# A polysketch attention and mixture-of-experts kernel: the second matmul of the mixture by Strassen's seven half products, its sums on GpSimd, and a rebuilt beginning

## Chip, cores, metric

One core of one Trainium2 chip; float32 in and out. The metric is device time in microseconds of the whole program, median of several executions. The program uses one core.

## The reference, cut to what matters

```python
# attention: B, H, S, D = 4, 4, 1088, 32; r = 8
#   phi(x) = outer product of S1 x and S2 x, 64 features; num / den by k_p, v and z sums
# its result, (B*S, H*D) = (4352, 128), is the x of the mixture
N, D, E, F = 4352, 128, 4, 1024
p = domain_probs / (domain_probs.sum(-1, keepdims=True) + 1e-09)
for e in range(E):
    h = np.maximum(x @ w1[e], 0.0)          # first matmul
    out += p[:, e:e + 1] * (h @ w2[e])      # second matmul
```

Hidden units come in 32 blocks of 128 (4 experts of 8). Per block and chunk of tokens the kernel makes hp = w1 x on TensorE, hid = max(hp, 0) * gate on VectorE, and adds w2 hid to an accumulator in PSUM on TensorE.

## The kernel before

Tokens are columns. Every 128x128 product is issued as two *half products* of 64 outputs each, on two column tiles of the array (I call them the two *sides*).

```python
def product(out, weights, moving, **flags):
    for r in (slice(0, 64), slice(64, P)):
        nc.tensor.matmul(out[r, :], weights[:, r], moving, **flags)
# ...
def first(i):
    m, kk = steps[i]                       # chunk, block
    hp = ps_h.tile([P, 512], F32, tag="h", name="hp")          # 2 buffers
    product(hp[:, 0:n], w1_sb[:, e, P * f : P * f + P], xT[chunks[m]][:, 0:n], start=True, stop=True)
    hid[i] = mpool.tile([P, CW], F32, tag="hid", bufs=4, name="hid")
    nc.vector.scalar_tensor_tensor(out=hid, in0=hp, scalar=0.0, in1=gate, op0=ALU.max, op1=ALU.mult)  # APs cut
def second(i):
    product(acc[m][:, 0:n], w2_sb[:, e, f, :], hid.pop(i)[:, 0:n], start=(kk == 0), stop=(kk == NK - 1))
# ...
for i in range(len(steps) + LA):           # LA = 2: second() runs two blocks behind first()
    first(i); second(i - LA); next(pieces, None)     # cut: conditions
```

`pieces` is a generator with the attention work of later chunks: each `next` issues one attention instruction (or a few on TensorE) among the mixture's. I call one such issue a *piece*. The names qp, qa, qf, qb (query features), kp (key features), yz and ev (the additions at the end of a chunk after the change) will turn up in the profiles below; gate is the weight of an expert for each token. In this kernel GpSimd makes the key products and is otherwise idle.

## Time and profile before

| | before |
|---|---|
| median in the first measurement (3 executions) | 537.84 us |
| span of the profile | 534.7 us |
| first hp | 27.1 us |
| from first hp to last acc | 504.0 us, TensorE busy 503.3 |
| busy PE / VectorE / GpSimd | 97% / 62% / 5% |

In the lines of the profile PE is TensorE, PEld its weight loads, DVE VectorE, ACT ScalarE, POOL GpSimd; L570 is line 570 of the kernel that ran; `a <- b` in a wait means that a stood still until b was done. "Busy" of TensorE counts the recorded, overlapping passes.

### The profile page before, as it was taken

To read this page: it belongs to the slowest core of one execution; us is meant where nothing else is said; L and a number is where in the kernel's file an instruction comes from. 1 tells how busy PE (TensorE), PEld (TensorE's weight loads), DVE (VectorE), ACT (ScalarE), POOL (GpSimd) and SP (SyncE) were. 2 spreads that over 40 slices of the span, in tenths; PEclk is the share of its full clock that TensorE was granted. 3 is DMA by queue.
4 is the path that set the end of the run, shared out by engine and by line. 5 is a ranking of instruction groups with operands and counts; after the bars stand their busy time and mean duration, and the time that the engine had idled before them with its cause. 6 is when DMAs were issued, how large, how long until landed. Compare 5 with 4: busy or idle time off the path is not lost.

```text
span 534.7 us, 9910 instructions
## 1 busy us (share of the span) xinstructions
PE 518.1 (97%) x4197; PEld 287.0 (54%) x4197; DVE 333.5 (62%) x788; ACT 25.3 (5%) x56; POOL 26.1 (5%) x80
## 2 busy tenths in 40 slices
PE   3799999999999999999999999999999999999997
PEld 1677776555554445544554445454555444444896
DVE  3878874777647645367866754447875664654554
ACT  1210000000000001000000000100000000000000
POOL 2240000000000004000000000400000000000000
PEclk9999999999999999999999999999999999999999
DMA  7492502002015002000202001100301000100100
GB/s 209 109 276 103 157 28 71 0 1 73 1 49 139 2 0 77 1 1 8 67 2 63 1 0 23 53 1 0 75 1 31 12 1 10 26 1 2 16 9 8
DMA packets 32893, 22.82 MB, mean 43 GB/s; under 512 B 21200, under 2 KB 29520, under 8 KB 32848
## 3 DMA queue, kind: packets, MB, share of 16 engines
q1 hardware_dynamic: 31536, 21.78, 14.7%
q8 instruction: 33, 0.54, 0.4%
q10 hardware_dynamic: 1312, 0.40, 0.4%
q14 instruction: 12, 0.10, 0.1%
HBM read 19.87 MB, written 2.31 MB: 41 GB/s over the span
## 4 chain that ended last, share of the span: by engine, by line
PE 95%; DVE 2%; DMA 1%; issue 1%; ACT 0%; SPq 0%; DVEq 0%; ACTq 0%
PE hp L141 44%; PE acc L141 44%; PE nd L141 3%; PE kv L141 1%; PE qc L141 1%; PE kf L141 1%; PE wp L146 1%; DMA kn<-in_k_dram 1%; DVE kp L287 1%; DVE den L399 0%; DMA vn<-in_v_dram 0%; DVE qp L374 0%; DVE fs L279 0%; DVE hid L492 0%; ACT den L389 0%
## 5 line engine op out<-in xcount | busy, mean ns | idle before, releaser
L492 DVE SCALAR_TENSOR_TENSOR hid<-hp,gate 128x384 f32<-128x384 f32 (+4 forms) x448 | 213.4, 476 | 185.4 <-PE hp L141 176.8
L141 PE MATMUL hp<-xT,w_sb 128*64 128x384 f32 (+4 forms) x1792 | 311.5, 426 | 1.2 <-DVE xT L404 1.0
L141 PE MATMUL acc<-hid,w_sb 128*64 128x384 f32 (+4 forms) x1792 | 311.0, 425 | 0.0
L141 PEld LDWEIGHTS acc<-hid,w_sb 128*64 128x64 f32 x1792 | 128.6, 137 | 106.9 <-issue 68.7
L141 PEld LDWEIGHTS hp<-xT,w_sb 128*64 128x64 f32 x1792 | 126.8, 137 | 106.0 <-issue 62.6
L287 POOL TENSOR_TENSOR kp<-fs 128x128 f32<-128x128 f32 (+1 forms) x56 | 22.6, 443 | 310.9 <-DVE fs L279 310.9
L399 DVE RECIPROCAL den<-den 128x128 f32<-128x128 f32 (+1 forms) x37 | 32.3, 876 | 0.2 <-ACT den L389 0.2
L389 ACT ACTIVATE den<-nd,eps 64x384 f32<-64x384 f32 (+4 forms) x28 | 14.4, 514 | 359.3 <-issue 313.4
L374 DVE TENSOR_TENSOR qp<-qa,qb 64x384 f32<-64x384 f32 (+4 forms) x56 | 26.6, 474 | 1.3
L141 PE MATMUL nd<-qp,kvz 128*64 128x384 f32 (+4 forms) x112 | 17.6, 427 | 0.7 <-DVE kvz L312 0.7
L371 DVE STREAM_SHUFFLE qa<-qf 128x384 f32<-128x384 f32 (+4 forms) x28 | 14.0, 502 | 0.0
L404 DVE TENSOR_TENSOR xT<-nd,den 64x384 f32<-64x384 f32 (+4 forms) x28 | 13.2, 473 | 0.5
L141 PEld LDWEIGHTS kv<-vx,kp 128*64 128x64 f32 (+1 forms) x288 | 11.9, 137 | 3.0 <-issue 2.0
L141 PE MATMUL kv<-vx,kp 128*64 128x66 f32 (+3 forms) x288 | 13.0, 238 | 0.0
L146 PE MATMUL wp<-warm 128*128 128x512 bf16 x13 | 4.3, 501 | 9.0 <-ACT warm L119 9.0
L141 PEld LDWEIGHTS nd<-qp,kvz 128*64 128x64 f32 x112 | 8.0, 137 | 8.0 <-issue 4.5
L141 PE MATMUL qc<-qT,sq 128*64 128x384 f32 (+4 forms) x56 | 9.8, 426 | 1.5 <-DVE fs L279 1.5
L141 PEld LDWEIGHTS kf<-sk,kT 128*64 128x64 f32 x144 | 8.2, 137 | 3.9 <-issue 2.6
L141 PE MATMUL kf<-sk,kT 128*64 128x128 f32 x144 | 9.8, 275 | 0.5 <-DVE fs L279 0.5
L354 DVE STREAM_TRANSPOSE qT<-qn 128x384 f32<-128x384 f32 (+4 forms) x14 | 6.9, 493 | 2.9 <-DMA qn<-in_q_dram 2.9
L146 PEld LDWEIGHTS <-warm 128*128 128x128 bf16 x13 | 1.5, 124 | 11.3 <-ACT warm L119 9.0
L274 ACT COPY fs<-kf 128x256 f32<-128x256 f32 (+1 forms) x12 | 3.8, 319 | 77.5 <-PE kf L141 77.5
(59 smaller groups left out, 64.5 us busy)
## 6 DMA issues: line engine op xcount, KB each, us to landing
gate<-gates SPq DMA_DIRECT2D x6, 768.0 KB, 4.3
w_sb<-in_moe_w_dram SPq DMA_DIRECT2D x8, 512.0 KB, 8.9
gate<-gates SPq DMA_DIRECT2D x4, 640.0 KB, 4.3
kn<-in_k_dram SPq DMA_DIRECT2D x4, 544.0 KB, 4.1
qn<-in_q_dram SPq DMA_DIRECT2D x4, 544.0 KB, 3.9
vn<-in_v_dram SPq DMA_DIRECT2D x28, 64.0 KB, 3.9
out_dram<-ob SPq DMA_DIRECT2D x24, 48.0 KB, 1.8
gate<-gates SPq DMA_DIRECT2D x2, 384.0 KB, 5.4
```

Source lines behind the costliest of these rows:

```text
L141: nc.tensor.matmul(out[r, :], weights[:, r], moving, **flags)
L146: nc.tensor.matmul(wp[:, :], warm[:, 0:P], warm[:, :], start=True, stop=True)
L274: nc.scalar.copy(fss[b][:, t0 : t0 + n, :], _ap(kf, 0, P, 0, [[P, n], [1, H * R2]]))
L287: eng.tensor_tensor(out=_ap(kps[b], 0, P, 256 * t0 + P * (h // 2) + 64 * x + 32 * (h % 2), [[256, n], [R, 4], [1, R]]), in0=_ap(fss[b], 0, ...
L354: nc.vector.transpose(qT[:, 0:n], qn[b][:, 32 * g0 : 32 * g0 + n])
L371: nc.vector.stream_shuffle(in_=qf[:, 0:n], out=qa[:, 0:n], mask=mask_a[x])
L374: nc.vector.tensor_tensor(out=qp[p][64 * x : 64 * x + 64, 0:n], in0=qa[64 * p : 64 * p + 64, 0:n], in1=qb[64 * p : 64 * p + 64, 0:n], op=A ...
L389: nc.scalar.activation(den[64 * p : 64 * p + 64, 0:n], nd[p][64 - 64 * p : 128 - 64 * p, 0:n], ACTF.Identity, bias=eps[64 * p : 64 * p + 6 ...
L399: nc.vector.reciprocal(den[:, s : s + w], den[:, s : s + w])
L404: nc.vector.tensor_tensor(out=xT[b, ch][r, 0:n], in0=nd[p][r, 0:n], in1=den[r, 0:n], op=ALU.mult)
L492: nc.vector.scalar_tensor_tensor(out=_ap(hid[i], 0, P, 0, [[32, n // 32], [1, 32]]), in0=_ap(hp, 0, P, 0, [[32, n // 32], [1, 32]]), scala ...
```

## The change

The intent: Strassen's scheme multiplies two 2x2 block matrices with seven block products for eight. Here the four weight blocks are two hidden blocks by two halves of the outputs, and the four blocks of hid are two hidden blocks by two halves of the columns. TensorE saves an eighth of the second matmul; in return there are four sums of weight blocks (once for each expert, GpSimd), four sums of hid blocks at every step (a *step* is now a pair of hidden blocks), and some additions at the end of a chunk (`gather`). The seven half products alternate between the two sides.

```diff
-    NK = E * FB
-    WIDTHS = [[192, 256, 320, 320], [384, 384, 320], [384, 384, 320], [384, 384, 192, 128]]
+    NQ = E * FB // 2
+    CHUNKS = [256, 416, 416] + [512] * 6 + [192]      # the last one stays plain
...
+    def first(i, work):
+        for j in range(2):
+            hp = psum(ps_h, "h")                       # 3 buffers
+            both(hp[:, 0:n], w1_sb[:, e, c : c + P], xT[...], start=True, stop=True)
+            nc.vector.scalar_tensor_tensor(out=hid[i] block j, in0=hp, in1=gate, ...)
+            work()                                     # a piece of attention
+        if plain(m):
+            return
+        nc.gpsimd.tensor_tensor(out=ts[:, 0:2, 0:w], in0=..., in1=..., op=ALU.subtract)   # two sums in one
+        nc.gpsimd.tensor_tensor(out=ts[:, 2, 0:w], in0=hid[i][:, 1, w:n], in1=ts[:, 0, 0:w], op=ALU.subtract)
+        (nc.vector if i % 2 else nc.gpsimd).tensor_tensor(
+            out=ts[:, 3, 0:w], in0=hid[i][:, 1, 0:w], in1=ts[:, 2, 0:w], op=ALU.subtract
+        )
...
+        todo = (      # second(): by side, (weights, moving); 3 or 4 of each are used in turn
+            [(blk(0, 0), hb(0, 0)), (new(3), hb(1, 1)), (blk(0, 1), hb(1, 0)), (new(1), tb(2))],
+            [(new(2), tb(1)), (new(0), tb(0)), (blk(1, 1), tb(3)), (new(1), tb(2))],
+        )
```

Cut from it: the beginning (the warm-up of TensorE no longer waits for ScalarE, q comes before v, query features of the first chunk as three replicated products in place of shuffles, key products straight from PSUM, some of them on GpSimd), the division (two 32x32 transposes around a small reciprocal), later key products on VectorE, chunks of 512, and the buffers that follow. The line with `nc.vector if i % 2` I call the *fourth sum*. In odd steps VectorE makes it, in the order of its program, ahead of the next step's hids, and it needs GpSimd's sums.

## The prediction

> **What bounds the kernel now.** I read the page first, its busy line and its chain.
>
> ```profile
> PE 518.1 (97%) x4197; PEld 287.0 (54%) x4197; DVE 333.5 (62%) x788; ACT 25.3 (5%) x56; POOL 26.1 (5%) x80
> ...
> PE 95%; DVE 2%; DMA 1%; issue 1%; ACT 0%; SPq 0%; DVEq 0%; ACTq 0%
> PE hp L141 44%; PE acc L141 44%; PE nd L141 3%; PE kv L141 1%; PE qc L141 1%; PE kf L141 1%; PE wp L146 1%; DMA kn<-in_k_dram 1%; DVE kp L287 1%; DVE den L399 0%; DMA vn<-in_v_dram 0%; DVE qp L374 0%; DVE fs L279 0%; DVE hid L492 0%; ACT den L389 0%
> ```
>
> TensorE is 95% of the chain that ends last, half of it each in the two mixture products, hp and acc. Busy alone does not prove saturation, so I asked for three stretches: the mixture, the end and the beginning (columns: PE, PEld, DVE, ACT, POOL busy).
>
> ```profile
> 27.10:531.10 504.00, 503.32 (x4032) 276.79 (x4032) 316.51 (x725) 19.72 (x42) 18.93 (x48) 1.00 0.13 37
> 531.10:534.80 3.70, 0.00 (x0) 0.00 (x0) 0.32 (x1) 0.00 (x0) 0.00 (x0) 0.88 0.12 18
> 0.00:27.10 27.10, 14.78 (x167) 10.19 (x167) 16.63 (x62) 5.61 (x14) 7.19 (x32) 1.00 0.58 158
> ```
>
> So the span is 27.1 us of beginning, 504 us in which TensorE never rests, and a tail of 3.7. The pace inside the middle comes from the timeline of TensorE:
>
> ```profile
> 300.42 0.81 PE L141 MATMUL hp<-xT,w_sb 128*64 128x384 f32 x4
> 301.07 0.81 PE L141 MATMUL acc<-hid,w_sb 128*64 128x384 f32 x4
> 301.71 0.81 PE L141 MATMUL hp<-xT,w_sb 128*64 128x384 f32 x4
> 302.36 0.81 PE L141 MATMUL acc<-hid,w_sb 128*64 128x384 f32 x4
> ```
>
> One 128x128 product of 384 columns is two half products (64 outputs each), recorded as two passes each, and the next begins 0.645 us later with no gap. The beginning, TensorE alone:
>
> ```profile
> 8.99 4.30 PE L146 MATMUL wp<-warm 128*128 128x512 bf16 x13 [8.99 <-ACT warm L119]
> 13.22 2.47 PE L141 MATMUL kf<-sk,kT 128*64 128x128 f32 x36
> 17.24 0.55 PE L141 MATMUL qc<-qT,sq 128*64 128x192 f32 x4 [1.55 <-DVE fs L279]
> 17.59 4.82 PE L141 MATMUL kv<-vx,kp 128*64 128x132 f32 x72
> 23.10 1.06 PE L141 MATMUL nd<-qp,kvz 128*64 128x192 f32 x8 [0.69 <-DVE kvz L312]
> 24.09 1.97 PE L141 MATMUL kf<-sk,kT 128*64 128x128 f32 x32
> 27.09 0.87 PE L141 MATMUL hp<-xT,w_sb 128*64 128x192 f32 x8 [1.03 <-DVE xT L404]
> ```
>
> The warm-up waits until 8.99 for a ScalarE instruction that stands behind the v loads in ScalarE's queue; everything follows from there.
>
> **What the Trainium skill says.** "TensorE: Matmul & The Clock Gate", section Back-to-back issue gap, gives N/2.4 + 2.5 ns for a warm matmul. The trace agrees if a pass of float32 counts two cycles a column: means of 486 ns at 384 columns and 273 at 128 differ by 0.832 ns a column, 2/2.4, and 0.645 us for four passes on two column tiles is 2 x (320 + 2.5). "TensorEngine Tiling (Array Packing)", section Key Properties, says that different tiles can execute weight loads and matmuls in parallel; that 0.645 us holds four passes of over 320 ns each agrees. "GPSIMD Engine Reference", section 3.1, has 4497 ns for a two-input add of 2048 elements, 2.2 ns an element. "SBUF — State Buffer", section Who interferes with whom, says that a VectorE instruction with two SBUF inputs contends with a GpSimd one that reads SBUF. The groups by form bear on both:
>
> ```profile
> L287 POOL TENSOR_TENSOR kp<-fs 128x160 f32<-128x160 f32 x28 | 12.2, 471 | 0.3 <-DVE fs L279 0.3
> L287 POOL TENSOR_TENSOR kp<-fs 128x128 f32<-128x128 f32 x28 | 10.6, 416 | 310.6 <-DVE fs L279 310.6
> L492 DVE SCALAR_TENSOR_TENSOR hid<-hp,gate 128x384 f32<-128x384 f32 x192 | 106.8, 556 | 117.6 <-PE hp L141 116.2
> L287 DVE TENSOR_TENSOR kp<-fs 128x160 f32<-128x160 f32 x4 | 2.0, 567 | 0.0
> ```
>
> GpSimd shows (471-416)/32 = 1.72 ns an element, a little better than the page. VectorE's two-input kp, run beside GpSimd's, takes 567 ns for 160 elements, as long as its 384-column hid, whose other input is PSUM: contention, as the page says.
>
> **The change, part by part.** A half product of n columns costs its side 2 x (0.833 n + 2.5) ns, from the above; a side is one column tile, and both run at once.
>
> *First product*, kept: 32 blocks x 4352 columns x 1.667 ns = 232.1 us, plus 10 chunks x 32 x 2 x 2.5 ns = 1.6: 233.7.
> *Second product*: 16 pairs of blocks, each seven half products of n/2 columns, 3.5 a side, in place of eight. On 4160 tokens: 16 x 3.5 x 2080 x 1.667 ns = 194.1 us, plus 9 x 16 x 7 x 2.5 ns = 2.5: 196.6. The last 192 tokens stay plain: 10.4. Together the mixture is 440.7 us.
> *Before, the same sum*: 64 x 4352 x 1.667 = 464.2, plus 14 x 64 x 2 x 2.5 ns = 4.5: 468.7. **Saved on TensorE: 28 us**, 7/8 of one product, little lost to the shorter matmuls. As TensorE never rests there, this counts whole if no other engine takes over.
>
> *Attention inside the mixture*: 5 ns a token (qc one product, nd two), kf 2.0 and kv 2.6 us a batch (2 x 1.3 by the timeline). Before: 896 tokens, one batch without kf, two whole: 32.6. After: 832 tokens and three whole batches: 34.5. Check on before: 27.1 + 468.7 + 32.6 = 528.4 against 531.1 read, so 2.7 us escape this count (row-tile changes in kv, waits between); I carry them over.
>
> *VectorE*: a hid of 512 columns, by the slope (556-291)/256 = 1.035 ns from the 384 and 128 forms, takes 690 ns, 320 instructions in all and some 195 us against 213. Added: one of four sums in every second step (about 0.42 us at 256 columns, 72 times, 30 us), the gathering of nine chunks (about 2.9 us each, 26 us), key products moved from GpSimd. The division gets cheaper: 32 us of den reciprocals become two transposes. About 380 us in a span near 505: not a bound by busy time.
> *GpSimd*: at 512 columns a step takes a sum of 512 elements (416 + 384 x 1.72 = 1.08 us), one of 256 (0.64) and, in even steps, a third: 2.0 us mean against a step of 2 x 0.858 + 3.5 x 0.432 = 3.2 us on TensorE. Not the bound, and with second() two steps behind first() the chain hid, three sums (about 2.5 us after the last hid) has nearly 5 us before TensorE wants it.
>
> *Beginning*: the warm-up no longer waits for ScalarE. kn landed at 5.2 and the three kT transposes ended at 6.6, with sk to be had by then: kf starts near 7 instead of 13.2. The three replicated query products cost 2.6 us of TensorE but take the shuffles away. Estimate: kf to 9.5, query products to 12.2, kv to 14.8, nd 16.3, division 17.7. The first gates have to pass behind 1.5 MB of weights, so I put the first hp, or the first hid that really goes through, at **19.8**, 7.3 us earlier, though with the first kf of batch 1 no longer tucked in.
>
> Sum: 19.8 + 440.7 + 34.5 + 2.7 carried + 3.3 for new waits + 3.7 tail = 504.7 us of span. The median stands 3.1 over the span of the profile (537.84 to 534.7), so **508 us**, 5.6% faster.
>
> **Rivals.** (1) *VectorE becomes the bound by its order.* In odd steps it does the fourth sum itself and must wait for GpSimd's two, about 1.5 us of standing still after the last hid. Two steps: 4 hid at 0.61 (issue spacing), 0.34 for the sum, some 1.5 of attention, 0.3 gathering, 1.5 waiting, 0.3 contention, 6.4 us against 7.0 of TensorE with its attention. Close: if contention adds 0.5 us an instruction instead, VectorE rules while attention is dense (about seven chunks, 56 pairs of steps) and 30 us could shrink to 10: 525. For it speak the 567 ns above; against it, that hid has one SBUF input and that most waits fall into slack. (2) *The first chunk starves.* At 256 columns a step is 1.63 us, while GpSimd has 1.27 plus weight sums of 0.64: 1.9 in the steps that have one. Worth 1 to 4 us, of which I counted about 2: 511 at worst. (3) *Pairing breaks.* Seven is odd and sides alternate across steps; were two neighbours to land on one side, or different moving data on two sides to slow each other, the 8-for-7 gain of 28 us would go: 536. The code alternates without exception; no case of two different streams exists in this trace, except in time between products. (4) *Beginning hidden anyway*: gates or v arrive late and hp starts at 25: 513.
>
> **Range and chances.** All waits hidden and hp at 18 gives 500; rival 1 by half, or 2 and 4 together, 517. So 500 to 517. Faster by over 2% means under 527.3, which only rival 1 in full with another, or 3, prevents: 0.94 faster, 0.05 same, 0.01 slower.
>
> **What would show it.** acc becomes 2016 recorded passes of 256, 208 and 128 columns beside the plain ones, starting on each side every 216 ns at 256; TensorE busy over 97% from first hp to last acc; first hp between 18 and 21; GpSimd busy near 290 us (96 steps of 2.0, 32 of 1.8, 16 of 1.3, weight sums and beginning 20); VectorE 360 to 410 with idle before the fourth sum near 1.5 us. I am wrong if waits of TensorE on sums or hid add up to more than 10 us, if GpSimd's 512-element sum takes over 1.6 us, or if the acc passes at 256 start more than 230 ns apart.

## The result

| | before | after |
|---|---|---|
| median, same measurement (4 executions each) | 537.77 us | 558.0 us |
| ratio, 95% interval | | 1.038 (1.036 to 1.040) |
| first hp / first hid | 27.1 / 27.7 us | 16.9 / 20.4 us |
| VectorE, GpSimd busy | 333, 26 us | 344, 350 us |

Ratios are the mean time of one kernel's fast runs over that of the other's of the same rounds, so not quite the ratio of the medians. The kernel became 20 us slower where 30 us faster was predicted. The page after, busy line and chain:

```profile
PE 512.1 (92%) x4178; PEld 301.8 (54%) x4178; DVE 344.4 (62%) x736; ACT 27.8 (5%) x67; POOL 349.8 (63%) x414
...
POOL 44%; DVE 31%; PE 17%; issue 4%; DMA 2%; POOLq 0%; DVEq 0%; SPq 0%
POOL sums L570 24%; DVE hid L557 16%; POOL sums L576 13%; PE h L169 8%; PE o L169 7%; POOL sums L577 6%; DVE sums L577 4%; PE f L169 3%; DVE qp L393 2%; DVE yz L661 1%; DVE ev L672 1%; DMA gates<-pt 1%; DVE qa L451 1%; DVE ob L635 1%; DMA gate<-gates 1%
```

TensorE went from 95% of the chain to 17%; GpSimd and VectorE share three quarters of it, with the sums and the hids, though each of them is busy for less than two thirds of the span. Two engines that are each a third idle and yet fill the chain in turn: that is the picture of a hand-over, not of a full engine. The three stretches, as before (window in us, its length, PE, PEld, DVE, ACT, POOL busy with the number of instructions, granted clock, DMA share, GB/s):

```profile
16.90:552.90 536.00, 498.67 (x3988) 292.99 (x3988) 332.86 (x685) 23.19 (x54) 338.38 (x372) 0.99 0.13 36
552.90:556.70 3.80, 0.16 (x1) 0.00 (x0) 0.38 (x1) 0.00 (x0) 0.00 (x0) 1.00 0.16 26
0.00:16.90 16.90, 13.22 (x190) 8.78 (x190) 11.20 (x50) 4.57 (x13) 11.38 (x42) 1.00 0.71 206
```

The beginning is 10 us shorter; the middle has 37 us in which no pass is running at all. Who waits for whom there (total us, times, longest):

```profile
DVE sums L577 <- POOL sums L576: 169.8, 72, 3.8
POOL sums L570 <- DVE hid L557: 154.8, 88, 5.3
...
PEld h L169 <- DVE hid L557: 58.9, 58, 2.9
...
PE h L169 <- DVE hid L557: 19.7, 23, 2.4
```

VectorE stands still for the fourth sum 72 times, 2.36 us on average; GpSimd stands still for hid nearly as long (154.8 us in 88 waits); and TensorE waits for hid, because hp has three PSUM buffers and only a hid frees one. It hardly waits for sums: only some 2.5 us of its waits name them. One turn late in the kernel, where no attention is left, first GpSimd and then VectorE (start, length, and in brackets the idle time before):

```profile
470.42 1.27 POOL L570 TENSOR_TENSOR sums<-hid 128x512 f32<-128x512 f32 x1 [1.74 <-DVE hid L557]
471.77 0.73 POOL L576 TENSOR_TENSOR sums<-hid,sums 128x256 f32<-128x256 f32 x1
472.58 0.72 POOL L577 TENSOR_TENSOR sums<-hid,sums 128x256 f32<-128x256 f32 x1
473.26 1.27 POOL L570 TENSOR_TENSOR sums<-hid 128x512 f32<-128x512 f32 x1
474.61 0.73 POOL L576 TENSOR_TENSOR sums<-hid,sums 128x256 f32<-128x256 f32 x1
477.08 1.28 POOL L570 TENSOR_TENSOR sums<-hid 128x512 f32<-128x512 f32 x1 [1.74 <-DVE hid L557]
```
```profile
469.66 1.96 DVE L557 SCALAR_TENSOR_TENSOR hid<-h,gate 128x512 f32<-128x512 f32 x3
475.37 0.43 DVE L577 TENSOR_TENSOR sums<-hid,sums 128x256 f32<-128x256 f32 x1 [3.75 <-POOL sums L576]
475.71 1.88 DVE L557 SCALAR_TENSOR_TENSOR hid<-h,gate 128x512 f32<-128x512 f32 x3
```

Five sums of two steps follow each other on GpSimd (470.42 to 475.34). VectorE is done with its hids at 471.62, stands still for 3.75 us before the fourth sum, does it at 475.37, then makes the next hids, and only after the second of them may GpSimd begin again, at 477.08. The turn is closed: 4.92 us of GpSimd and 1.74 in which VectorE works and GpSimd waits, **6.66 us for two steps**, and none of it can start before the part ahead of it has ended. TensorE needs 2 x 3.23 = 6.45 us for two steps, by the prediction's pace; so even without attention the turn is the longer, and every piece, gathering addition or conflict between the two engines inside it makes it longer still: from fourth sum to fourth sum the last three turns of chunk 8 took 6.64 to 6.67 us, those of chunks 3 to 7 7.4 to 7.8 on average. I call it the **ring**.

TensorE's own part is as predicted. Four lines of its timeline in the same kernel, two passes that start together and the two that follow:

```profile
387.10 0.38 PE L169 MATMUL o<-sums,w2s 128*64 128x256 f32 x1
387.11 0.38 PE L169 MATMUL o<-hid,w2s 128*64 128x256 f32 x1
387.32 0.38 PE L169 MATMUL o<-sums,w2s 128*64 128x256 f32 x1
387.33 0.38 PE L169 MATMUL o<-hid,w_sb 128*64 128x256 f32 x1
```

Passes of 256 columns start on both sides together, with different weights and different moving data, and the next pair 0.216 us later.

Two theories went to the chip. **Ring**: the order of the fourth sum on VectorE closes a cycle between two in-order engines, and its length sets the time. **Throughput**: GpSimd, at 350 us busy, and its conflicts with VectorE's two-input instructions are simply too much. (That the sums reach TensorE too late was a third.) The first calls for a change of order, the second for less work.

### The profile page after: what moved, and what is told of

Read it like the earlier page. It is cut to its first block, busy times and chain, and to the rows that moved or that the text cites. A ratio compares the mean times of both kernels' runs of the same rounds, so it can differ in the third digit from the quotient of the medians.

```text
span 556.7 us, 9898 instructions
## 1 busy us (share of the span) xinstructions
PE 512.1 (92%) x4178; PEld 301.8 (54%) x4178; DVE 344.4 (62%) x736; ACT 27.8 (5%) x67; POOL 349.8 (63%) x414
## 4 chain that ended last, share of the span: by engine, by line
POOL 44%; DVE 31%; PE 17%; issue 4%; DMA 2%; POOLq 0%; DVEq 0%; SPq 0%
POOL sums L570 24%; DVE hid L557 16%; POOL sums L576 13%; PE h L169 8%; PE o L169 7%; POOL sums L577 6%; DVE sums L577 4%; PE f L169 3%; DVE qp L393 2%; DVE yz L661 1%; DVE ev L672 1%; DMA gates<-pt 1%; DVE qa L451 1%; DVE ob L635 1%; DMA gate<-gates 1%
## 5 line engine op out<-in xcount | busy, mean ns | idle before, releaser
L169 PE MATMUL h<-xT,w_sb 128*64 128x512 f32 (+3 forms) x1280 | 315.9, 536 | 25.0 <-DVE hid L557 19.7
L570 POOL TENSOR_TENSOR sums<-hid 128x512 f32<-128x512 f32 (+2 forms) x144 | 177.4, 1232 | 158.8 <-DVE hid L557 154.8
L169 PE MATMUL o<-sums,w2s 128*64 128x256 f32 (+2 forms) x864 | 208.8, 359 | 1.2 <-POOL w2s L473 1.2
L557 DVE SCALAR_TENSOR_TENSOR hid<-h,gate 128x512 f32<-128x512 f32 (+3 forms) x320 | 186.9, 599 | 29.9 <-PE h L169 24.8
L169 PEld LDWEIGHTS h<-xT,w_sb 128*64 128x64 f32 x1280 | 120.7, 137 | 115.8 <-DVE hid L557 58.9
L169 PE MATMUL o<-hid,w_sb 128*64 128x256 f32 (+3 forms) x704 | 178.5, 353 | 0.0
L169 PEld LDWEIGHTS o<-sums,w2s 128*64 128x64 f32 x864 | 115.3, 137 | 53.7 <-issue 27.0
L577 DVE TENSOR_TENSOR sums<-hid,sums 128x256 f32<-128x256 f32 (+2 forms) x72 | 31.3, 434 | 169.8 <-POOL sums L576 169.8
L576 POOL TENSOR_TENSOR sums<-hid,sums 128x256 f32<-128x256 f32 (+2 forms) x144 | 102.2, 710 | 11.3
L169 PEld LDWEIGHTS o<-hid,w_sb 128*64 128x64 f32 x704 | 92.4, 137 | 20.3 <-issue 13.6
L169 PE MATMUL o<-hid,w2s 128*64 128x256 f32 (+2 forms) x288 | 79.8, 359 | 0.8 <-POOL w2s L473 0.8
L577 POOL TENSOR_TENSOR sums<-hid,sums 128x256 f32<-128x256 f32 (+2 forms) x72 | 52.3, 726 | 5.7
```

Of the source, the lines that this page charges most:

```text
L169: nc.tensor.matmul(out(s), weights(s), moving(s), **flags)
L557: nc.vector.scalar_tensor_tensor(out=_ap(hid[i], 0, P, CW * j, [[32, n // 32], [1, 32]]), in0=_ap(hp, 0, P, 0, [[32, n // 32], [1, 32]]), ...
L570: nc.gpsimd.tensor_tensor(out=ts[:, 0:2, 0:w], in0=_ap(hid[i], 0, P, w, [[CW, 2], [1, w]]), in1=_ap(hid[i], 0, P, 0, [[w, 2], [1, w]]), op ...
L576: nc.gpsimd.tensor_tensor(out=ts[:, 2, 0:w], in0=hid[i][:, 1, w:n], in1=ts[:, 0, 0:w], op=ALU.subtract)
L577: (nc.vector if i % 2 else nc.gpsimd).tensor_tensor(out=ts[:, 3, 0:w], in0=hid[i][:, 1, 0:w], in1=ts[:, 2, 0:w], op=ALU.subtract)
```

## The experiments

Each run is an edit of the changed kernel. I also read the length of each chunk in each trace, from its first hid to the next chunk's first hid; the table is below.

### 1. The fourth sum deferred

```diff
-        (nc.vector if i % 2 else nc.gpsimd).tensor_tensor(out=ts[:, 3, 0:w], ...)
+        if i % 2: waiting.append(lambda: fourth(nc.vector))   # issued after the next step's two hids
+        else:     fourth(nc.gpsimd)
```

> Only the place of VectorE's fourth sum (odd steps) in its program order changes: it is issued after the two hids of the next step, so VectorE no longer stands still for GpSimd before it may make the next hids. Theory, a ring: in the changed kernel GpSimd's five sums of two steps (about 4.9 us) and then VectorE's fourth sum and two hids (about 1.7 us plus an attention instruction between them) follow each other without overlap, 6.65 us per two steps at the least and over 8 where attention is dense, against 6.45 of TensorE plus its attention. With the ring cut, TensorE is the bound again: about 505 us (500 to 515), waits of VectorE on the second sum near zero. Rival, throughput or contention of GpSimd and VectorE (350 and 344 us busy, two-input instructions blocking each other): the order of one instruction changes nothing, 545 to 558 us.

513.6 us, correct, ratio to before 0.956 (0.954 to 0.958). The same instructions in another order: 44 us less than the changed kernel. VectorE's wait on the second sum fell from 169.8 us to

```profile
DVE sums L583 <- POOL sums L580: 6.0, 6, 2.1
```

while GpSimd was busy longer (356 us) in a shorter span. Throughput as the only cause is out.

### 2. All four sums on GpSimd

```diff
-        (nc.vector if i % 2 else nc.gpsimd).tensor_tensor(
+        nc.gpsimd.tensor_tensor(
```

> The fourth sum always on GpSimd: no VectorE instruction waits for GpSimd any more, but GpSimd gets 72 more sums of 0.7 us, some 50 us more work (busy about 400 us). Ring theory: GpSimd needs 2.85 us per step of 512 columns against 3.5 of TensorE, so it is hidden: 505 to 515 us. Rival, GpSimd's throughput: it was the bound, so it gets slower: 565 us or more.

513.0 us, correct, 0.955 (0.953 to 0.957). GpSimd has 52 us more to do (402 busy) and the kernel is 45 us faster. No instruction of VectorE that lies ahead of a hid reads GpSimd's sums any more, and the chain is TensorE's again (GpSimd had 44% of it in the changed kernel):

```profile
PE 88%; POOL 7%; DMA 3%; DVE 1%; issue 1%; DVEq 0%; POOLq 0%; SPq 0%
```

The trace still puts 24 us of waits before 17 hids down to GpSimd's sums. Why was not looked into; the chunk table (experiment 8) shows no cost of them from chunk 2 on.

### 3. No sums at all

```diff
-        ts = mpool.tile(...)            # and the three instructions that fill it
-        tb = lambda a: ts[:, a, 0:w]
+        tb = lambda a: hb(a // 2, 1 - a % 2)     # slices of hid: wrong on purpose
```

> Wrong result on purpose: none of the four sums of hid is computed, the seven half products read slices of hid instead. TensorE's instructions stay the same in number and size. It measures what TensorE's part of the change is worth: if the seven half products run in pairs as predicted (28 us saved, first hp at 16.9), 500 to 505 us. Rival: TensorE itself is slower than predicted with different streams on its two column tiles: 520 or more.

503.9 us (the result is wrong, as meant), 0.938 (0.936 to 0.939). This is what TensorE, beginning, attention and gathering cost together, within the 500 to 505 expected. The prediction without its 3.3 us for new waits had 504.5.

### 4. One piece moved

```diff
-            work()                      # after each of the two hids
+            if i % 2: work()
+            elif j:   work(); work()    # even steps: both pieces after the second hid
```

> In even steps the attention instruction that stood between the two hids is issued after the second one; nothing else changes, same work on each engine. Ring theory: that one instruction lay in the ring (about 0.5 us in some 55 to 60 pairs of steps, more where it was blocked by GpSimd), so 20 to 30 us less: 528 to 540 us. Rival (throughput, contention): no work is removed, 553 to 560 us.

558.0 us: **no change**, and my expectation missed. The trace shows why the simple ring was too simple. There are two ways round. One is the five sums, fourth sum, two hids. The other is VectorE's own: four hids with all pieces ahead of the last one, then GpSimd's first two sums of the odd step, then the fourth sum. The piece lies on both; moving it behind the second hid takes it off the first way and leaves it on the other. In a dense stretch of this run GpSimd, done with the even step's sums at 250.0, stood idle until the odd step's hid was made and began its next sum only at 251.5. The pieces also collide with GpSimd's sums, and that lengthens now the one and now the other. Two qp of VectorE, and the sums of GpSimd that ran at the same time:

```profile
242.64 0.55 DVE L393 TENSOR_TENSOR qp<-qa,qb 64x384 f32<-64x384 f32 x1
247.34 1.22 DVE L393 TENSOR_TENSOR qp<-qa,qb 64x384 f32<-64x384 f32 x1
```
```profile
242.69 1.64 POOL L574 TENSOR_TENSOR sums<-hid 128x512 f32<-128x512 f32 x1
246.87 1.27 POOL L574 TENSOR_TENSOR sums<-hid 128x512 f32<-128x512 f32 x1 [1.74 <-DVE hid L557]
```

At 242.6 the qp had begun first and kept its 0.55 us, and the sum took 1.64 in place of 1.27. At 247.3 the sum had begun first and kept its 1.27, and the qp took 1.22. So moving a piece may only move the conflict; how much of the 558.0 us is conflict this run does not tell.

### 5. The fourth sum on VectorE in every step

```diff
-        (nc.vector if i % 2 else nc.gpsimd).tensor_tensor(
+        nc.vector.tensor_tensor(
```

> The fourth sum on VectorE in every step, in order, so GpSimd has 72 sums less to do (about 300 us busy instead of 350) and VectorE 72 more. Ring theory: now every step is one ring: two hids (1.2 us and 0.16 to GpSimd), GpSimd's two sums (1.35 and 0.8), the fourth sum (0.35), 3.85 us at 512 columns without attention, some 0.5 more for each attention instruction between, against 3.2 of TensorE: 570 to 595 us, though GpSimd has less to do. Rival, GpSimd's throughput or its contention with VectorE: less GpSimd work means faster, under 550 us.

638.1 us, 1.187 (1.185 to 1.189). GpSimd's load fell to 294 us, and the kernel got 80 us slower: the sharpest answer against throughput. The size was more than the 570 to 595 that I had said, since I had counted chunks of 512 only. The first three chunks took 46.2, 61.3 and 62.6 us, where the run without sums has 28.0, 48.2 and 45.9: 48 us more, so the ring is longer than TensorE's work there too. A turn without attention is as expected; VectorE late in the run:

```profile
561.33 0.43 DVE L577 TENSOR_TENSOR sums<-hid,sums 128x256 f32<-128x256 f32 x1 [2.19 <-POOL sums L576]
561.67 1.28 DVE L557 SCALAR_TENSOR_TENSOR hid<-h,gate 128x512 f32<-128x512 f32 x2
565.14 0.42 DVE L577 TENSOR_TENSOR sums<-hid,sums 128x256 f32<-128x256 f32 x1 [2.19 <-POOL sums L576]
```

From fourth sum to fourth sum 3.81 us, one step, against 3.2 of TensorE.

### 6. More look-ahead

```diff
-    LA = 2                  # hid 4 buffers, sums 3
+    LA = 3                  # hid 5, sums 4
```

> The changed kernel with the second product three steps behind the first instead of two (one more buffer for hid and sums). Ring theory: the ring of VectorE and GpSimd does not contain the second product, so it stays at 553 to 560 us. Rival, the sums come too late for TensorE: one more step of 3.2 us of slack would hide them, 505 to 530 us.

555.0 us, 1.033 (1.030 to 1.036), within what the ring foresaw. A whole step more of slack for TensorE buys 3 us of 54; that the sums come too late for TensorE is not the cause.

### 7. Every chunk plain

```diff
     def plain(m):
-        return m == NC - 1
+        return True             # and each chunk is stored as the last one is
```

> The changed kernel with every chunk as its last one: eight half products, no sums of hid, no gathering; beginning, chunk widths, attention as changed. It splits the change into Strassen and the rest. From the run without sums (503.9) and the 28 us predicted for the eighth half product: 530 to 534 us. If the rebuilt beginning gave nothing: 537 or more.

530.3 us, correct, 0.988 (0.985 to 0.991). The rebuilt beginning with the other chunk widths and the new attention is worth 7 us by itself. Against this run, seven half products with no sums are 26.4 us faster (503.9), and the change as it came is 27.7 us slower.

### 8. All sums on GpSimd, first chunk plain

```diff
-        return m == NC - 1
+        return m in (0, NC - 1)         # on top of experiment 2
```

> All sums on GpSimd, and the first chunk (256 tokens) plain, so that GpSimd has only the weight sums to do in it. In the run with all sums on GpSimd the chunks of 512 took as long as without any sum; only the first chunk took 36.5 us instead of 28.0. If that is GpSimd's load of weight sums and hid sums, this gives back 8.5 less 1.7 for the eighth half product: 505 to 508 us. If it is the late weights or gates, it stays at 511 to 515.

506.8 us, correct, 0.943 (0.941 to 0.946): the fastest correct version, 30 us under before and 51 under the changed kernel. The chunk table shows what was left after experiment 2 (us from the first hid of a chunk to the first hid of the next, or to the last hid for chunk 9):

| chunk (tokens) | as changed | deferred | all on GpSimd | no sums | all on GpSimd, first plain |
|---|---|---|---|---|---|
| 0 (256) | 41.5 | 35.8 | 36.5 | 28.0 | 29.3 |
| 1 (416) | 52.6 | 48.8 | 48.6 | 48.2 | 49.0 |
| 2 (416) | 53.2 | 46.6 | 45.9 | 45.9 | 45.5 |
| 3 (512) | 60.9 | 57.1 | 57.3 | 57.3 | 57.3 |
| 4 (512) | 63.8 | 56.8 | 56.8 | 56.8 | 56.9 |
| 5 (512) | 62.8 | 57.5 | 57.3 | 57.3 | 57.3 |
| 6 (512) | 61.9 | 56.2 | 55.9 | 55.5 | 55.9 |
| 7 (512) | 58.6 | 56.0 | 54.6 | 54.6 | 54.6 |
| 8 (512) | 55.2 | 51.1 | 51.1 | 51.1 | 51.1 |
| 9 (192) | 20.6 | 21.9 | 21.8 | 21.9 | 21.8 |

From chunk 2 on, the version with every sum on GpSimd takes as long as the version with none, within 0.4 us. The sums *and* their conflicts with VectorE are then hidden entirely. Chunk 0 is the exception: its steps are short, and the weight sums of experts 1 to 3 stand in GpSimd's queue between its sums (which of the two weighs more was not separated). One chunk in which TensorE does the eighth half product takes them in.

### 9. Pieces moved into the wait

```diff
-            work()                          # after each hid
+            if m == 0 or plain(m): work()
+            elif j:                         # after the second hid: one in even steps, three in odd ones
+                for _ in range(3 if i % 2 else 1): work()
```

> The fourth sum stays in order on VectorE; only attention instructions move, from the second chunk on: none between two hids, one after the second hid of an even step, three after the second hid of an odd step, where VectorE waits for GpSimd anyway (2.1 us at 512 columns). Same work, same waits in the program. The ring theory as the moved-piece run corrected it: two ways round, GpSimd's five sums with fourth sum and two hids (6.66 us) and VectorE's four hids with every attention instruction ahead of the last hid and two sums of GpSimd; the move takes both below 7.0 us of TensorE. Expected 518 to 540 us, not the 503.9 of no sums, since three attention instructions in a row wait for each other through TensorE. Rival, the amount of work or the two-input contention sets the time: 553 to 560 us.

545.1 us, 1.014 (1.012 to 1.016): 13 us less than as changed with nothing removed, so the position of the pieces in the turn matters, as the two ways round say and throughput by itself does not. But it is short of the 518 to 540 expected. The trace shows the pieces paying in the wait: two qp beside GpSimd's sums took 1.30 and 0.99 us (at 236.9 and 238.2) in place of 0.55, and the fourth sum, which could have begun at 238.8, came at 239.2. How the rest of the shortfall divides between such conflicts and pieces that wait for each other through TensorE I did not separate.

### 10. Deferred, first chunk plain

```diff
+        waiting.append(...)                 # experiment 1
+        return m in (0, NC - 1)             # and the plain first chunk
```

> The fourth sum of odd steps on VectorE but deferred by one step, and the first chunk plain. Deferring alone gave 513.6 with 35.8 us for the first chunk and 56 to 57.5 for the dense ones; a plain first chunk took 29.3: 506 to 509 us, no better than the version with all sums on GpSimd (506.8). If GpSimd's 50 us less were worth something: under 505.

508.0 us, 0.945 (0.944 to 0.947), as expected and no better than experiment 8 (506.8), which leaves VectorE 43 us freer (331 busy for 374). Where the deferred sum is issued it meets GpSimd's sums: its mean in experiment 1 is 857 ns at 256 columns against 425 in the changed kernel, where GpSimd was idle beside it. That costs nothing that shows.

## Why the prediction was wrong, point by point

- **TensorE saved 28 us: right, within 2 us.** Seven half products for eight in the same frame are worth 26.4 us (530.3 to 503.9, with the gathering paid for). The passes start 216 ns apart at 256 columns, as computed; two sides with different data do not slow each other. Rival 3, broken pairing, is out.
- **The beginning: right in sum.** First hp came at 16.9, where the division alone was put at 17.7 and 18 to 21 was named as the sign, but the first hid only at 20.4, held 3.5 us by the gates; the text had put "the first hp, or the first hid that really goes through," at 19.8 because of the gates, and that part held. The tail of 3.7 came out as 3.8.
- **The sum without new waits was 504.7 - 3.3 us of span plus 3.1: right.** That is 504.5, and the run without sums has 503.9. Part of this closeness is luck. The 3.1 set the median of three runs against the span of another, profiled run, whose own time was 536.49: the true gap was 1.8. The span without sums was 502.1 where 501.4 had been worked out. The two slips run against each other. Two smaller ones stand in the text: the attention after the change adds up to 34.3 by its own rates, not 34.5, and a gain of 10 us would be 528, not the 525 of rival 1.
- **The step that failed is the term "3.3 for new waits".** It should have been 53.5: the measured 558.0 less those 504.5. The runs put it at 54.1, as changed less no sums. Behind it stands rival 1, which the prediction had named and then dismissed with "6.4 us against 7.0 of TensorE". Three things in that line failed:
  1. *"1.5 waiting".* It took GpSimd as idle when the odd step's hid arrives. It was still at the even step's three sums. The measured wait is 2.36 us on average and 3.75 in the turn shown.
  2. *The sums' sizes.* GpSimd's sum of 512 elements was put at 1.08 us and that of 256 at 0.64, by the slope of kp, whose operands repeat elements. Measured: 1.27 and 0.73 alone, 1.35 and about 0.75 with spacing and conflicts. The prediction had worked out 2.2 ns an element from the figure of "GPSIMD Engine Reference", section 3.1, of the Trainium skill; I preferred the trace of another access pattern.
  3. *The shape of the sum.* VectorE's two steps and GpSimd's two steps were each added up and compared with TensorE. What had to be added was one walk round the cycle, across both engines: 4.92 + 1.74 = 6.66 us bare, where two engines at 62 and 63% busy looked harmless. Bare, that is over the 6.45 of TensorE without attention, but still under the 7.0 with it. What put it over 7.0 as well are the pieces, the gathering and the conflicts that stand inside the walk: chunk 4 took 63.8 us, 7.98 for two steps, against 7.10 without sums. The "nearly 5 us" that the look-ahead gave were slack of TensorE's second product, and the ring does not pass through it (experiment 6).
- **Contention as the reason for rival 1: not by itself.** The prediction let "contention adds 0.5 us an instruction" decide whether VectorE rules. Conflicts are about as large as that (a qp of 1.22 us for 0.55, a fourth sum of 857 ns for 425), but with the ring cut they cost nothing that shows from chunk 2 on (chunk table). Inside the closed ring they do lengthen the turn; their share was not measured.
- **Rival 2, the first chunk: right in kind, too small.** 1 to 4 us had been allowed; 8.5 of its 13.5 us loss stay when the ring is cut (36.5 for 28.0), and go when the chunk is plain.
- **The signs named in advance** did their work: TensorE's waits for hid were over the 10 us named, and the idle before the fourth sum was 2.36 us for "near 1.5"; both pointed to rival 1. Three other forecasts missed: TensorE 93% busy from first hp to last acc (498.67 of 536.00) for over 97%, GpSimd 350 us busy for near 290 (point 2 above), VectorE 344 for 360 to 410.

That the order of the fourth sum caused the loss is shown: cut in two different ways it gives back 44 and 45 us, made denser it costs 80 more. Of the 9 to 10 us that stay after either cut (513.0 and 513.6 for 503.9), 8 to 9 lie in chunk 0. How each piece and conflict lengthens the turn is only partly shown (experiments 4 and 9 both missed their numbers).

## What to carry to other kernels

When two engines hand work back and forth, look for a cycle: an instruction that waits for the other engine and stands, in program order, ahead of what that other engine needs next. Add up one walk round it across both engines and compare that with the bound; busy shares of 62% and 63% say nothing against it. Cutting a cycle by order, here one instruction issued a step later or given to the engine it waits for, can be worth more than removing work, and more look-ahead outside the cycle bought 3 us of 54 here.

## What the Trainium skill lacked or had wrong

- "TensorE: Matmul & The Clock Gate", section Architectural detail, says in passing that ScalarE's and VectorE's queues, and in its way GpSimd's, are strictly first in, first out. The trace agrees: VectorE stood still for 3.75 us ahead of the fourth sum, though the hp of the next hid had been finished for over a microsecond (its last pass by 474.3, its hid at 475.71). Of the pages cited here, none draws the consequence, that the queues of two engines can form a ring whose length bounds the kernel: 558.0 us with it and 513.0 without.
- "GPSIMD Engine Reference", section 3.1: the estimate of 2.2 ns an element from its 4497 ns for a two-input add of 2048 elements holds better than the 1.72 read from kp: 1271 ns at 512 elements and 727 at 256 are 2.13 ns an element and 183 ns fixed. It has no figure for kp's product, whose operands repeat elements and which is quicker (628 ns at 256, mean of two in the changed kernel); whether the repeating or the multiplication does that, no run here separates.
- "SBUF — State Buffer", section Who interferes with whom: right on the conflict (yz, two inputs of SBUF, at 512 columns 678 ns on average in the run without sums and 1091 in the changed kernel). It lacks how little this can matter where neither engine is the bound: chunk 3 took 57.3 us with all sums on GpSimd and with none.
- "TensorE: Matmul & The Clock Gate" has, in the section Back-to-back issue gap, no figure for float32 on two column tiles: here 0.216 us for each recorded pass of 256 columns on each side, both sides at once, with different moving data.
